# Sharing PSUM banks between small score matmuls in a fused Nyström-attention and MoE kernel

## The chip, the cores and the metric

The kernel runs on one core of one Trainium2 chip. The time is device microseconds of one execution of the whole program; the figure quoted for a kernel is the median of its runs. The engines are TensorE (PE in the rows; its weight loads are listed apart), VectorE (DVE), ScalarE (ACT), GpSimd (POOL) and the queues that issue transfers (SP above all).

## The reference, cut to what matters

Eight batches with eight heads of 576 x 64 go through Nyström attention with 32 landmarks per head, and then two gated layers without softmax follow:

```python
q_lm = q.reshape(B, H, 32, 18, D).mean(axis=3)       # landmarks: means of 18 neighbours
k_lm = k.reshape(B, H, 32, 18, D).mean(axis=3)
A  = softmax(scale * q    @ k_lm.T)                  # 576 x 32 per head
Bm = softmax(scale * q_lm @ k_lm.T)                  # 32 x 32
C  = softmax(scale * q_lm @ k.T)                     # 32 x 576
Z  = Bm.T / (norm1(Bm) * norminf(Bm) + 1e-6)
for _ in range(6):
    Z = 2 * Z - Z @ Bm @ Z                           # Newton steps
attn = A @ Z @ C @ v
x = ((attn @ w1) * (attn @ w2)) @ w3 @ w_out         # first layer
h = x @ w_in
out = elu(h) @ w_out2                                # second layer
```

All of it is float32; the large products are made of float32r halves, three matmuls for one product.

## The kernel before

The program has three stretches. In the first (to about 160 us) the weights are unpacked on ScalarE, VectorE and GpSimd (`conv_job`), a product of two weights is formed (`w3acc`), and the attention of batch 0 is worked out. In the second (to about 620 us) the first layer runs over 128 units: unit u is 12 matmuls `ab` (scores A times the folded matrix `m`) and, two units later, 12 matmuls `y`. Each has 288 columns. In the third the second layer runs (`h`, `o`), which the change doesn't touch.

In the second stretch the attention of batch b+1 is made between the units of batch b. A table of half steps, `steps`, says which piece goes where. With i the unit within a batch (0 to 15), the loop does: `ab(u)`; `quick`, which takes the Newton steps; `ab_product` (copy on ScalarE, product `g` on VectorE); `ab_split` of the unit before (`gl` on VectorE); `fill` with half step 2i; `yy(u-2)`; `fill` with half step 2i+1. So a piece at an even half step stands on TensorE between `ab` and `y`, and one at an odd half step between `y` and the next `ab`. Each engine works off its own queue in the order in which this was written. Every `fill` ends with a step of a weight conversion for the second layer (four instructions `w_y`, `w_p`, `w_p`, `w_s` on VectorE in some of the steps; products and splits on GpSimd).

The pieces that matter here, all of one batch's attention:

- `b_scores`, half step 6: landmark scores `bs`, eight small matmuls; VectorE takes the maximum (`bmx`) and the difference (`bm`). `b_exp` (7) and `b_soft` (8) finish the softmax.
- `c_scores`, 7 and 8: landmark queries against keys (`c`), each time eight matmuls of 288 columns into two PSUM banks; ScalarE copies them to `e`.
- `newton` 13 to 18 (`n`), and `cv` 18 and 19: C times v, one half of the heads each; VectorE scales both into `cvbd`.
- `zcv`, 21: Z times that (`z`), eight small matmuls, one copy on VectorE.
- `a_scores`, 22 and 26: keys' landmarks against queries (`a`), into two banks; VectorE transposes them.
- `m_tiles`, 24 and 28 (and 0 and 2 of the next batch): the matrix `m`, whose weights are `z`.

All these use one PSUM pool, `ps_at`, of two banks of 512 columns that are handed out in turn. A matmul into a bank that is handed out anew waits until the last reader of the bank's former content is done. `bs` takes 64 columns of a bank, `z` 128, a half of `c` or `a` 288.

Of the kernel before, what the change touches and what calls it, by code (L numbers as in the profile page):

```python
# [22 lines left out]
ML = 32  # L23
R = S // ML
NP = H // 2
NH = S // 2
# [36 lines left out]
def nystrom_moe_kernel(ctx, tc, qT, kT, vm, vr, w12, w3T, w_out1, w_in2, w_out2, out):  # L63
    nc = tc.nc
    pe, dve, act, pool, sp = nc.tensor, nc.vector, nc.scalar, nc.gpsimd, nc.sync
# [132 lines left out]
    qpad = att.tile([128, 2, NP, ML], F32, name="qpad")  # L198
    cvbd = att.tile([128, NP, 128], F32, name="cvbd")

    loaded = {}
# [19 lines left out]
    class Attention:  # L221
# [24 lines left out]
            for i in range(2):  # L246
                act.copy(qpad[64 * i : 64 * i + 64, i], self.qsum[64 * i : 64 * i + 64])

        def pair_scores(self, nm, small, big, cols):


            ps = [self.ps(f"{nm}{i}") for i in range(2)]
            for hp in range(NP):
                for i in range(2):
                    sl = slice(64 * i, 64 * i + 64)
                    pe.matmul(  # L256
                        ps[i][32 * hp : 32 * hp + 32, : cols.stop - cols.start],
                        small[sl, hp, :], big[sl, hp, cols], start=True, stop=True,
                    )
            return ps  # L260

        def c_scores(self, n):
            if n == 0:
                self.e = [self.t([128, S], f"e{blk}") for blk in range(2)]
            cols = slice(n * NH, (n + 1) * NH)
            for e, p in zip(self.e, self.pair_scores(f"c{n}", self.qsum, loaded[self.b]["k"], cols)):
                act.copy(e[:, cols], p[:, :NH])

        def c_max(self, blk):
# [16 lines left out]
            dve.reciprocal(self.crs.rearrange("p a o -> p (a o)"), s)  # L286

        def b_scores(self):
            p = self.ps("bs")
            for i in range(2):  # L290
                for hp in range(NP):
                    pe.matmul(
                        p[32 * hp : 32 * hp + 32, i * ML : (i + 1) * ML], qpad[:, i, hp, :], self.ksum[:, hp, :],
                        start=True, stop=True,
                    )
            pv = p[:, : 2 * ML].rearrange("p (a m) -> p a m", m=ML)
            mx = self.t([128, 2, 1], "bmx")
            dve.tensor_reduce(mx.rearrange("p a o -> p (a o)"), pv, axis=AX.X, op=ALU.max)
            bm = self.t([128, 2, ML], "bm")
            dve.tensor_tensor(bm, pv, mx.to_broadcast([128, 2, ML]), op=ALU.subtract)  # L300
            self.bm = bm

        def b_exp(self):
            act.activation(self.bm, self.bm, AF.Exp, scale=SC2)
# [94 lines left out]
                    )  # L399

        def zcv(self):
            p = self.ps("z")
            for hp in range(NP):
                for i in range(2):
                    pe.matmul(
                        p[64 * i : 64 * i + 64, hp * ML : (hp + 1) * ML], cvbd[:, hp, 64 * i : 64 * i + 64],
                        self.X[:, i, ML:], start=True, stop=True,
                    )
            self.z = self.t([128, NP, ML], "z")
            dve.tensor_copy(self.z.rearrange("p a m -> p (a m)"), p[:, : NP * ML])  # L410

        def m_tiles(self, jn):
            ps = self.pair_scores(f"m{jn}", self.z, w12_sb, slice(jn * 512, (jn + 1) * 512))
# [5 lines left out]
                M_hi[self.b, jn, blk] = hi  # L419
                M_lo[self.b, jn, blk] = lo  # L420

        def a_scores(self, n):
            t = self.t([128, 2 * SEG, ML], "at")
            tf = t.rearrange("p k m -> p (k m)")
            ps = self.pair_scores(f"a{n}", self.ksum, loaded[self.b]["q"], slice(n * NH, (n + 1) * NH))
            for blk, p in enumerate(ps):
                dve.transpose(tf[:, blk * NH : (blk + 1) * NH], p[:, :NH])
            self.at = t
# [32 lines left out]
        def steps(self, first=False):  # L461

            s = {}

            def at(i, f, *a):
                s.setdefault(i, []).append((f, a))

            for hp in range(NP):
                at((-16, -14, -12, -11)[hp], self.sums, "k", hp)
                at(hp, self.sums, "q", hp)  # L470
            at(4, self.q_pad)
            at(6, self.b_scores)
            at(7, self.b_exp)
            at(7, self.c_scores, 0)
            at(8, self.c_scores, 1)
            at(8, self.b_soft)
            at(9, self.c_max, 0)
            at(9, self.c_exp, 0)
            at(10, self.b_norms)
            at(10, self.c_max, 1)  # L480
            at(10, self.c_exp, 1)
            at(11, self.b_norms2)
            at(12, self.r0)
            at(13, self.c_norm)
            for k in range(6):
                at(13 + k, self.newton, k)
            for k in range(3):
                at(11 + 2 * k, self.c_trans, k)
            at(18, self.cv, 0)
            at(19, self.cv, 1)  # L490
            at(21, self.zcv)
            when = ((22, 22, 23, 24, 25, 26, 27), (26, 27, 28, 29, 30, 32, 34))
            if first:
                when = ((11, 11, 12, 13, 14, 15, 16), (17, 17, N1, N1 + 1, N1 + 2, N1 + 3, N1 + 4))
            for n, o in enumerate(when):
                at(o[0], self.a_scores, n)
                at(o[1], self.a_max)
                at(o[2], self.a_sub)
                at(o[3], self.a_exp)
                at(o[4], self.a_sum)  # L500
                at(o[5], self.a_mul, n)
                at(o[6], self.a_split, n)
            return s
# [6 lines left out]
    with tc.manual_schedule():  # L510
# [55 lines left out]
        for o in ORDER:  # L566
            if o == "A":
                k, n_wo = n_wo, n_wo + 1
# [25 lines left out]
        a0, st0 = atts[0], steps[0]  # L594
# [8 lines left out]
        i = 0  # L603
# [191 lines left out]
        for u in range(nu + LAG):  # L795
            if u < nu:
                b, n, fc = units[u]
                i = n * K1 + fc
# [35 lines left out]
        for u in range(LAG, n2 + LAG2):  # L834
            if u < n2:
                i, f = units2[u]
# [59 lines left out]
```

## Time and profile before

| | us |
|---|---|
| three runs | 1472.49, 1472.89, 1474.19 (median 1472.89) |
| the profiled execution | 1474.1 |
| its span | 1472.3 |
| TensorE busy | 1417.4 |
| VectorE busy | 887.3 |
| ScalarE busy | 696.1 |
| GpSimd busy | 252.4 |

TensorE is busy for 96% of the span. Its idle time lies in the first stretch; between 200 and 600 us the page shows hardly any. A busy TensorE can still lose time: matmuls are pipelined, and it is the distance between their starts that says how fast they go. VectorE is busy for some 75% of the second stretch. GpSimd works in the first two stretches alone.

### The profile page before, as it was taken

What the parts mean: (1) busy time and instruction counts of PE and PEld (TensorE: products, weight loads), DVE (VectorE), ACT (ScalarE), POOL (GpSimd) and SP (SyncE); (2) the same over time, 40 slices, a digit from 0 to 9 for tenths busy, and PEclk for the clock granted to TensorE, in tenths of its full rate; (3) what the DMA queues carried; (4) which work ended last, traced back from release to release, by engine and by line L of the source; (5) the groups of instructions that cost most, each with busy time, mean ns of one, the idle gap of its engine ahead of it and who ended that gap; (6) DMA issues with size and microseconds to landing.
All of it is one profiled execution on the core that took longest, in us unless ns stands there. A gap on an engine that the chain in (4) does not pass through costs nothing.

```text
span 1472.3 us, 23676 instructions
## 1 busy us (share of the span) xinstructions
PE 1417.4 (96%) x9552; PEld 1144.7 (78%) x9552; DVE 887.3 (60%) x1719; ACT 696.1 (47%) x1333; POOL 252.4 (17%) x231
## 2 busy tenths in 40 slices
PE   5786899999999999999999999999999999999998
PEld 2234788888888888898888888888888888888886
DVE  8988686877878786634545445454444545445443
ACT  5664444545454544334445444454444544445443
POOL 5554324243423434201000000000000000000000
PEclk9888999999999999999999999999999999999999
DMA  7553244454433333236310010100101000010000
GB/s 292 182 187 118 78 153 154 140 176 148 173 135 139 135 139 117 79 144 231 128 50 8 0 57 1 58 0 0 58 1 57 1 30 29 0 58 0 30 1 29
DMA packets 40302, 129.46 MB, mean 88 GB/s; under 512 B 3840, under 2 KB 12032, under 8 KB 35072
## 3 DMA queue, kind: packets, MB, share of 16 engines
q1 hardware_dynamic: 37888, 111.16, 21.5%
q0 software_dynamic: 2304, 16.78, 2.9%
q8 instruction: 75, 1.23, 0.3%
q14 instruction: 35, 0.29, 0.1%
HBM read 92.27 MB, written 35.65 MB: 87 GB/s over the span
## 4 chain that ended last, share of the span: by engine, by line
PE 90%; DVE 7%; issue 1%; ACT 1%; DMA 1%; SPq 0%; DVEq 0%; ACTq 0%
PE o L751 9%; PE o L753 9%; PE o L752 9%; PE h L723 9%; PE h L722 9%; PE h L724 9%; PE y L663 5%; PE ab L636 5%; PE ab L637 4%; PE ab L638 4%; PE y L665 4%; PE y L664 4%; PE m L256 2%; PE w3acc L524 2%; PE n L357 1%
## 5 line engine op out<-in xcount | busy, mean ns | idle before, releaser
L751 PE MATMUL o<-w,eh 128*128 128x512 f32 x576 | 227.0, 394 | 0.7 <-ACT ysb L669 0.7
L723 PE MATMUL h<-yl,w 128*128 128x512 f32 x576 | 227.0, 394 | 0.0
L753 PE MATMUL o<-w,el 128*128 128x512 f32 x576 | 226.9, 394 | 0.0
L752 PE MATMUL o<-w,eh 128*128 128x512 f32 x576 | 226.8, 394 | 0.0
L722 PE MATMUL h<-yh,w 128*128 128x512 f32 x576 | 226.4, 393 | 0.0
L724 PE MATMUL h<-yh,w 128*128 128x512 f32 x576 | 226.3, 393 | 0.0
L732 DVE SCALAR_TENSOR_TENSOR t<-m,t 128x512 f32<-128x512 f32 x144 | 99.7, 693 | 196.2 <-ACT m L731 196.2
L68 ACT CAST eh<-t 128x512 fp32r<-128x512 f32 x144 | 89.4, 621 | 213.7 <-DVE t L733 213.7
L663 PE MATMUL y<-gh,w3oh 128*128 128x288 f32 x512 | 160.6, 314 | 1.5 <-DVE w3ol L69 1.5
L69 DVE TENSOR_TENSOR el<-t,eh 128x512 fp32r<-128x512 f32 x144 | 99.7, 692 | 98.8 <-ACT eh L68 98.8
L636 PE MATMUL ab<-ath,mh 128*128 128x288 f32 x512 | 157.5, 308 | 1.2 <-DVE g L647 1.2
L637 PE MATMUL ab<-atl,mh 128*128 128x288 f32 x512 | 152.5, 298 | 0.0
L638 PE MATMUL ab<-ath,ml 128*128 128x288 f32 x512 | 151.8, 297 | 0.0
L665 PE MATMUL y<-gh,w3ol 128*128 128x288 f32 x512 | 151.3, 296 | 0.0
L664 PE MATMUL y<-gl,w3oh 128*128 128x288 f32 x512 | 151.2, 295 | 0.1
L728 ACT COPY hs<-h 128x512 f32<-128x512 f32 x144 | 84.4, 586 | 100.0 <-PE h L724 99.9
L751 PEld LDWEIGHTS o<-w,eh 128*128 128x128 f32 x576 | 108.2, 188 | 26.2 <-ACT ysb L669 1.1
L723 PEld LDWEIGHTS h<-yl,w 128*128 128x128 f32 x576 | 108.0, 188 | 25.6
L722 PEld LDWEIGHTS h<-yh,w 128*128 128x128 f32 x576 | 108.0, 188 | 25.4
L753 PEld LDWEIGHTS o<-w,el 128*128 128x128 f32 x576 | 108.1, 188 | 25.2
L724 PEld LDWEIGHTS h<-yh,w 128*128 128x128 f32 x576 | 108.1, 188 | 25.1
L752 PEld LDWEIGHTS o<-w,eh 128*128 128x128 f32 x576 | 108.2, 188 | 24.7
(132 smaller groups left out, 2417.2 us busy)
## 6 DMA issues: line engine op xcount, KB each, us to landing
wd<-w2c SPq DMA_DIRECT2D x32, 512.0 KB, 3.4
w<-wd POOLq DMA_DIRECT2D x16, 1024.0 KB, 14.3
k<-in_kT_dram SPq DMA_DIRECT2D x8, 1152.0 KB, 7.3
q<-in_qT_dram SPq DMA_DIRECT2D x8, 1152.0 KB, 6.1
yd<-ysb SPq DMA_DIRECT2D x16, 576.0 KB, 3.7
yin<-yd SPq DMA_DIRECT2D x36, 256.0 KB, 4.0
out_dram<-osb SPq DMA_DIRECT2D x36, 256.0 KB, 2.2
w_raw<-in_w3T_dram SPq DMA_DIRECT2D x16, 512.0 KB, 5.2
```

What stands on the lines that cost most here:

```text
L636: pe.matmul(p[:, :NH], mh[:, cs], ah[:, blk, :], start=(blk == 0), stop=False)
L637: pe.matmul(p[:, :NH], mh[:, cs], al[:, blk, :], start=False, stop=False)
L638: pe.matmul(p[:, :NH], ml[:, cs], ah[:, blk, :], start=False, stop=(blk == 1))
L663: pe.matmul(a[oc][:, :NH], w3o_hi[fc][:, os_], gh, start=(fc == 0), stop=False)
L664: pe.matmul(a[oc][:, :NH], w3o_hi[fc][:, os_], gl, start=False, stop=False)
L665: pe.matmul(a[oc][:, :NH], w3o_lo[fc][:, os_], gh, start=False, stop=(fc == K1 - 1))
L722: pe.matmul(p[:, :TB], w2[f][:, 0, kk * 128 : (kk + 1) * 128], yhi[:, kk, :], start=(kk == 0), stop=False)
L723: pe.matmul(p[:, :TB], w2[f][:, 0, kk * 128 : (kk + 1) * 128], ylo[:, kk, :], start=False, stop=False)
L724: pe.matmul(p[:, :TB], w2[f][:, 1, kk * 128 : (kk + 1) * 128], yhi[:, kk, :], start=False, stop=(kk == KD - 1))
L751: pe.matmul(a, eh[:, ts_], w2[f][:, 2, :], start=(f == 0), stop=False)
L752: pe.matmul(a, eh[:, ts_], w2[f][:, 3, :], start=False, stop=False)
L753: pe.matmul(a, el[:, ts_], w2[f][:, 2, :], start=False, stop=(f == K2 - 1))
```

## The change

Three pieces move, and two pairs of pieces share a bank.

`b_scores` no longer stands at half step 6; it is called by `c_scores(0)` at half step 7, takes the last 64 columns of a bank, and hands that bank on as the first of the two into which the keys' scores go (columns 0 to 287). `b_exp` goes from 7 to 8 and `b_soft` from 8 to 9. `cv(1)` goes from 19 to 18, right behind `cv(0)`, which stands behind the last Newton step. `zcv` goes from 21 to 22 for all batches but the first: it is called by `a_scores(0)`, takes the last 128 columns of a bank, and hands it on as the first bank of the queries' scores.

```diff
-        def pair_scores(self, nm, small, big, cols):
+        def pair_scores(self, nm, small, big, cols, ps=None):
-            ps = [self.ps(f"{nm}{i}") for i in range(2)]
+            ps = ps or [self.ps(f"{nm}{i}") for i in range(2)]
...
         def c_scores(self, n):
-            for e, p in zip(self.e, self.pair_scores(f"c{n}", self.qsum, loaded[self.b]["k"], cols)):
+            ps = [self.b_scores()] + [self.ps("c0")] if n == 0 else None
+            for e, p in zip(self.e, self.pair_scores(f"c{n}", self.qsum, loaded[self.b]["k"], cols, ps)):
...
         def b_scores(self):
             p = self.ps("bs")
+            o = 512 - 2 * ML
-                        p[32 * hp : 32 * hp + 32, i * ML : (i + 1) * ML], qpad[:, i, hp, :], self.ksum[:, hp, :],
+                        p[32 * hp : 32 * hp + 32, o + i * ML : o + (i + 1) * ML], qpad[:, i, hp, :], self.ksum[:, hp, :],
-            pv = p[:, : 2 * ML].rearrange("p (a m) -> p a m", m=ML)
+            pv = p[:, o:].rearrange("p (a m) -> p a m", m=ML)
...
+            return p
...
         def zcv(self):
-            p = self.ps("z")
+            p = self.zp = self.ps("z")
+            o = 512 - NP * ML
-                        p[64 * i : 64 * i + 64, hp * ML : (hp + 1) * ML], cvbd[:, hp, 64 * i : 64 * i + 64],
+                        p[64 * i : 64 * i + 64, o + hp * ML : o + (hp + 1) * ML], cvbd[:, hp, 64 * i : 64 * i + 64],
-            dve.tensor_copy(self.z.rearrange("p a m -> p (a m)"), p[:, : NP * ML])
+            dve.tensor_copy(self.z.rearrange("p a m -> p (a m)"), p[:, o:])
...
-        def a_scores(self, n):
+        def a_scores(self, n, with_z=False):
+            ps = None
+            if with_z:
+                self.zcv()
+                ps = [self.zp, self.ps("a0")]
-            ps = self.pair_scores(f"a{n}", self.ksum, loaded[self.b]["q"], slice(n * NH, (n + 1) * NH))
+            ps = self.pair_scores(f"a{n}", self.ksum, loaded[self.b]["q"], slice(n * NH, (n + 1) * NH), ps)
...
-            at(6, self.b_scores)
-            at(7, self.b_exp)
             at(7, self.c_scores, 0)
+            at(8, self.b_exp)
             at(8, self.c_scores, 1)
-            at(8, self.b_soft)
+            at(9, self.b_soft)
...
             at(18, self.cv, 0)
-            at(19, self.cv, 1)
-            at(21, self.zcv)
+            at(18, self.cv, 1)
+            if first:
+                at(21, self.zcv)
...
-                at(o[0], self.a_scores, n)
+                at(o[0], self.a_scores, n, not first and n == 0)
```

Three places show what this does to the queues. TensorE before, in the attention of batch 5: the product `z` stands between `y` and `ab`, the queries' scores `a` one block of `ab` later (`ath`, `mh`, `ml` are the halves of the operands of `ab`; a `w3o` row is a `y` matmul).

```order
L665 MATMUL y_5910<-gh_5737,w3ol_93 128x288
L405 MATMUL z_5923<-X_5791,cvbd 64x32 x8
L636 MATMUL ab_0_5943<-ath_5266,mh_1_0_5122 128x288
...
L638 MATMUL ab_1_5950<-ath_5266,ml_1_0_5123 128x288
L636 MATMUL ab_1_5950<-ath_5266,mh_1_1_5125 128x288
L637 MATMUL ab_1_5950<-atl_5267,mh_1_1_5125 128x288
L638 MATMUL ab_1_5950<-ath_5266,ml_1_1_5126 128x288
L256 MATMUL a_5_5966<-q_5128,ksum_4713 32x288
L256 MATMUL a_5_5967<-q_5128,ksum_4713 32x288
```

The same place on TensorE after the change, with the semaphores that each row waits for:

```order
L648 MATMUL ab_1_5929<-ath_5257,ml_1_1_5117 128x288
L411 MATMUL z_5944<-X_5781,cvbd 64x32 [waits PE_49]
L411 MATMUL z_5944<-X_5781,cvbd 64x32 x7
L256 MATMUL z_5944<-q_5119,ksum_4705 32x288 [waits DMAHW2_49,DVE_49]
L256 MATMUL a_5_5955<-q_5119,ksum_4705 32x288 [waits PE_49]
```

All 12 `ab` rows now stand ahead of `z`, nothing stands between `z` and the first score matmul, and that matmul, which writes into z's bank, waits for VectorE: the count that it waits for is the one that the copy of `z` raises. The queue of VectorE at that place, before and then after (`k` to `ksum` are the landmark sums of a later batch, `at` the transposed scores):

```order
L241 TENSOR_REDUCE ksum_5741<-k_5595 128x32
L410 COPY z_5932<-z_5923 128x128
L241 TENSOR_REDUCE ksum_5741<-k_5595 128x32
L138 TENSOR_SCALAR w_y<-w_y 128x512
L143 TENSOR_SCALAR w_p<-w_y 128x512
L146 SCALAR_TENSOR_TENSOR w_p<-w_raw,w_p 128x512
L148 TENSOR_SCALAR w_s<-w_p 128x512
L647 TENSOR_TENSOR g_5959<-ab_1_5950,a_5957 128x288
L69 TENSOR_TENSOR gl_5901<-g_5898,gh_5900 128x288
L427 STREAM_TRANSPOSE at_5965<-a_5_5966 128x288
```

```order
L241 TENSOR_REDUCE ksum_5731<-k_5585 128x32 x2
L138 TENSOR_SCALAR w_y<-w_y 128x512
L143 TENSOR_SCALAR w_p<-w_y 128x512
L146 SCALAR_TENSOR_TENSOR w_p<-w_raw,w_p 128x512
L148 TENSOR_SCALAR w_s<-w_p 128x512
L657 TENSOR_TENSOR g_5938<-ab_1_5929,a_5936 128x288
L69 TENSOR_TENSOR gl_5891<-g_5888,gh_5890 128x288
L416 COPY z_5953<-z_5944 128x128
L437 STREAM_TRANSPOSE at_5956<-z_5944 128x288
```

The copy of `z` moved behind six instructions: the four of the conversion, `g` and `gl`. On TensorE the landmark scores stand so after the change:

```order
L675 MATMUL y_5335<-gh_5252,w3ol_94 128x288
L295 MATMUL bs_5392<-ksum_4705,qpad 32x32 [waits PE_49,Activation_49]
L295 MATMUL bs_5392<-ksum_4705,qpad 32x32 x3
L295 MATMUL bs_5392<-ksum_4705,qpad 32x32 [waits Activation_49]
L256 MATMUL bs_5392<-k_4559,qsum_5196 32x288 [waits DMAHW0_49,DVE_49]
L256 MATMUL c_5_5405<-k_4559,qsum_5196 32x288 [waits PE_49]
```

Before, 12 matmuls `y` stood between the eight `bs` and the first `c`. Now the first key score follows at once and waits for the difference `bm`, the last reader of `bs`.

## Rows read from the trace of the kernel before

**Rows 1.** The page: busy tenths of TensorE, and its granted clock, in 40 slices

```profile
PE   5786899999999999999999999999999999999998
PEclk9888999999999999999999999999999999999999
```

**Rows 2.** Timeline of TensorE, batch 5's z and a: start us, us, instruction

```profile
453.51 0.29 PE L665 MATMUL y<-gh,w3ol 128*128 128x288 f32 x1
453.73 0.66 PE L405 MATMUL z<-X,cvbd 128*64 128x32 f32 x16
454.32 0.40 PE L636 MATMUL ab<-ath,mh 128*128 128x288 f32 x1
454.56 0.30 PE L637 MATMUL ab<-atl,mh 128*128 128x288 f32 x1
...
455.89 0.29 PE L638 MATMUL ab<-ath,ml 128*128 128x288 f32 x1
456.11 0.72 PE L256 MATMUL a<-q,ksum 64*32 64x288 f32 x16
```

**Rows 3.** Timeline of TensorE, batch 5's bs and the last y behind it

```profile
421.20 0.33 PE L292 MATMUL bs<-ksum,qpad 128*32 128x32 f32 x16
...
423.02 0.29 PE L665 MATMUL y<-gh,w3ol 128*128 128x288 f32 x1
```

**Rows 4.** Timeline of VectorE behind that bs

```profile
422.41 0.21 DVE L298 TENSOR_REDUCE bmx<-bs 128x2 f32<-128x64 f32 x1
422.66 0.22 DVE L300 TENSOR_TENSOR bm<-bs,bmx 128x64 f32<-128x64 f32 x1
```

**Rows 5.** Timeline of VectorE around batch 5's z: idle time before, and its releaser, in brackets

```profile
452.67 0.45 DVE L69 TENSOR_TENSOR gl<-g,gh 128x288 fp32r<-128x288 f32 x1
...
454.44 0.29 DVE L410 COPY z<-z 128x128 f32<-128x128 f32 x1 [0.66 <-PE z L405]
454.65 0.74 DVE L241 TENSOR_REDUCE ksum<-k 128x32 f32<-128x576 f32 x1
...
457.73 0.29 DVE L148 TENSOR_SCALAR w_s<-w_p 128x512 uint16<-128x512 uint16 x1
457.94 0.45 DVE L647 TENSOR_TENSOR g<-ab,a 128x288 f32<-128x288 f32 x1
458.31 1.34 DVE L69 TENSOR_TENSOR gl<-g,gh 128x288 fp32r<-128x288 f32 x1
```

**Rows 6.** Timeline of GpSimd in the same microseconds

```profile
455.52 1.29 POOL L166 TENSOR_TENSOR w2c<-w_x,w2c 128x512 fp32r<-128x512 f32 x1
458.17 1.17 POOL L155 TENSOR_TENSOR w_t<-w_t,w_s 128x512 f32<-128x512 f32 x1 [1.35 <-DVE w_s L148]
```

**Rows 7.** Timelines of VectorE and TensorE where a matmul waited for the copy of z

```profile
116.85 0.29 DVE L410 COPY z<-z 128x128 f32<-128x128 f32 x1
...
117.19 1.96 PE L256 MATMUL m<-w_sb,z 64*32 64x512 f32 x16 [3.06 <-DVE z L410]
```

**Rows 8.** Timelines of TensorE and VectorE, batch 7's a, with no conversion on VectorE

```profile
591.07 0.71 PE L256 MATMUL a<-q,ksum 64*32 64x288 f32 x16
...
591.23 0.46 DVE L647 TENSOR_TENSOR g<-ab,a 128x288 f32<-128x288 f32 x1 [1.55 <-ACT gh L68]
```

**Rows 9.** Timeline of TensorE, first m of batch 2 and of batch 3

```profile
258.31 1.45 PE L256 MATMUL m<-w_sb,z 64*32 64x512 f32 x16
...
325.75 1.09 PE L256 MATMUL m<-w_sb,z 64*32 64x512 f32 x16
```

**Rows 10.** Timeline of VectorE in the first stretch, batch 0's landmark softmax

```profile
55.22 0.21 DVE L310 TENSOR_REDUCE bsum<-bm 128x2 f32<-128x64 f32 x1
...
56.58 0.93 DVE L313 TENSOR_TENSOR bm<-bm,bsum 128x64 f32<-128x64 f32 x1
59.58 0.69 DVE L69 TENSOR_TENSOR w3ol<-w3acc,w3oh 128x512 fp32r<-128x512 f32 x1 [2.06 <-ACT w3oh L68]
```

## The prediction

> **What bounds the kernel now.** I read the page first, then TensorE's timeline through one batch, then VectorE's and GpSimd's timelines beside it. TensorE is the bound from the sixth slice on, at full granted clock (a 9 is 90% or more) [rows 1]. Within the first layer its matmuls start every 0.13 us (454.56 to 455.89 is ten steps), and small groups interrupt them. Such a group costs more than its work: the gap into it is 0.22 us (453.51 to 453.73) and the second large matmul behind it comes 0.24 us after the first, where 0.13 is usual [rows 2]. That is 0.09 + 0.11 = 0.20 us at the two edges, and it is what a merged group can save. The z group as a whole moves the stream by 454.56 - 453.51 - 0.27 = 0.78 us. VectorE is not the bound in the stretch, but it is fed by TensorE and works in order, so the question is where in its queue a result stands for which TensorE now has to wait.
>
> **What is removed.** Per batch three interruptions: bs joins c, the second half of cv joins the first, z joins a. The work of each stays. In the second stretch the first merge counts for batches 2 to 7 (batches 0 and 1 have theirs before 160 us, where TensorE waits anyway), the two others for batches 1 to 7. For cv nothing waits that did not before, so 7 x 0.20 = 1.4 us are gained. Its bounds are 0 and 0.4 per merge (a change of tile form within the group may keep an edge, or more than the edges may go).
>
> **The wait behind bs.** Before, the 12 y between bs and c (from 421.46 to 423.02) covered VectorE's maximum and difference. Now c's first matmul writes the bank that they read, and queues behind them. In the new place bs runs after those y, about 422.8 to 423.1 on this clock; VectorE had by 422.41 reached bmx, so gl and all ahead of it are done and it is idle [rows 3, 4]. From the end of the group: 0.05 to VectorE's start (z ends at 453.73 + 0.66 = 454.39, its copy starts at 454.44 [rows 2, 5]), 0.25 to the second instruction, 0.22 for it [rows 4], 0.05 back to TensorE (117.14 to 117.19 [rows 7]): 0.57 us of wait. Everything on TensorE stands behind it, the next ab first. Less the edge saved, +0.37 us a batch; six batches give +2.2 us. Bounds per batch: 0.17 (if two edges' worth is saved) and 0.57 (nothing saved).
>
> **The wait behind z.** Here VectorE is not idle. Its copy of z now stands behind the conversion's four instructions, g and gl. I work batch 5 through. TensorE, without the z group, comes to the place of the a group 0.78 us earlier: z runs from 455.33 to 455.99, and the first a could follow then. VectorE, without the 0.66 us of waiting for z and the 0.21 to its next start, has the rest of its queue 0.87 us earlier: w_s at 456.86, g at 457.07, gl at 457.44 [rows 5]. It cannot be much earlier, since GpSimd's subtraction until 456.81 holds up just this kind of instruction [rows 6]. Behind w_s's start by 0.44 us GpSimd begins its next product (458.17 against 457.73), so at 457.30, for 1.17 us; the gl row that ran beside such a product took 1.34 us, one that did not 0.45 [rows 5, 6]. I take 1.34, because four of the five gl rows at this place (batches 2 to 6) are that long. A next instruction starts 0.08 before the recorded end, so the copy runs from 458.70 to 458.99 and a starts at 459.05. The wait is 459.05 - 455.99 = 3.06 us. With a gl of 0.45 the copy would run from 457.81 and a start at 458.16: 2.17 us.
>
> Batches 2 to 5 have the same queue: three at 3.06 and one at 2.17 make 2.84, less 0.20, times four: +10.6 us. Batches 1 and 6 have their conversion elsewhere against GpSimd's work, and batch 7 has none. Its rows give the least wait there can be: g starts 0.16 us behind the old start of a (591.07 and 591.23 [rows 8]); g and gl take a step of 0.37 each, the copy 0.29, the way back 0.06, so a could start at 592.32, and z would end at 591.73: 0.59 us. With a long gl it is 1.48. I take 1.0 for batch 7, less the edge +0.8, and the middle of 0.59 and 3.06, so 1.8, for batches 1 and 6, together +3.3 (rounded up). Sum for z: +14.7 us, with bounds of 7 x 0.39 = +2.7 and 7 x 2.86 = +20.
>
> **What the waiting gives back.** The first m of a batch stands on VectorE's transposes of a. Where VectorE came late, its group took 1.45 us and not 1.09 [rows 9]; four of the batches 1 to 7 show 1.41 to 1.45. When TensorE has waited for the copy, VectorE has caught up and the transposes follow a at once: -0.35 x 4 = -1.4 us. Bounds 0 and -1.7.
>
> **The first stretch.** Batch 0's four softmax instructions ran from 55.22 to 57.51 us, in time that VectorE then spent waiting (2.06 us) for ScalarE [rows 10]. Now they stand behind that work, before the maximum that the chain of waits goes through; I take 1.0 us, between 0.8 (each at its shortest) and 2.3. In batch 1 c's start moves behind one conversion, but VectorE sets the pace there: +0.2, at most 1.3. b_exp and b_soft one half step later cost nothing in the second stretch: b_soft at 9 still stands ahead of the norms at 10, and the first matmul that needs them comes at 12, with blocks of y and ab between. No transfer is moved.
>
> **Sum.** 2.2 + 14.7 - 1.4 - 1.4 + 1.2 = +15.3 us. Made against the profiled execution's 1474.1 us (span 1472.3) this is 1489.4; that execution stood 1.2 us above the median of the runs, so on the median it is 1488.2 us. About 0.2%, 3 us, is what a measurement here can tell from no change.
>
> **Two rules of the Trainium skill.** The rows show groups of different tile forms: 128*32 for bs, 128*64 for z, 64*32 for a [rows 2, 3]. The Trainium skill, "TensorEngine Tiling (Array Packing)", section Key Properties, says that changing the tiling mode, as against the tile, drains TensorE. By it the merges bs with c and z with a save no edge, and the sum is 13 x 0.20 = 2.6 us higher; no row of before shows these two neighbours.
>
> **Rivals.** First, TensorE doesn't really wait, since the shared bank's columns are apart: then 20 merges at 0.20 give -4.0 us, with the first stretch's 1.2 on top 1470 us. Against it speak the semaphore on the first score matmul in the built program, and the copy that raises it. The Trainium skill, "PSUM — Partial Sum Buffer", section "PSUM bank collisions raise a hardware error", says that two engines collide in a bank and quadrant even at disjoint columns, so by it no such matmul can be let go early; no run here shows that. I give this 3%.
>
> Second, faster: the waits are short and the merges give back the most they can. The price is 0.4 and not 0.20 a merge, which is what a bs group of 0.33 us would set free if nearly all of it ran under c's loading. Then 20 x 0.4 = 8.0 stand against 6 x 0.57 + 7 x 0.59 = 7.5 us of waits, and with m's 1.4 us it is about 1471 us. This decides as soon as a merge saves more than half the average wait. Against it: the edges measured are 0.20. Chance 4%.
>
> Third, short waits at edges of 0.20: the conversion comes out of z's way because VectorE runs ahead, all seven waits fall to 0.59, and m still gives back a part: 2.2 + 2.7 - 1.4 - 0.5 + 1.0 = +4.0, 1477 us. If m gives back its 1.4 and the first stretch nothing, it is +2.1, and that would measure as no change. For it: VectorE no longer loses the 0.66 us ahead of z's copy. Against it: GpSimd's rows, which hold VectorE up whenever it comes. Chance 14%, of which 8 within 0.2%.
>
> Fourth, TensorE's granted clock falls after waits of 3 us, as it does in the first slices [rows 1], where waits are longer: half speed for some microseconds in each of seven batches, 1500 us or more. The slices don't show to which wait, if any, a fall belongs. Chance 4%.
>
> **How the numbers follow.** The forecast, waits of about 2 to 3 us behind z and 0.57 behind bs, has 75%. Its own range is 1480 to 1496: with gl never held up (-3.6) and batches 1 and 6 at the least wait on one side, with every wait at 3.06, and 2.3 in the first stretch, on the other. Downwards the range takes in the third rival: 1477 to 1496. Faster by over 0.2% has the first two rivals, 6% with a little of each outside; within 0.2% 9%; slower 85%.
>
> **What would show it.** In the changed kernel's waits TensorE should have a row for a behind the copy of z, seven times, some 13 to 20 us in all, the longest near 3, and one for c behind bm of about 0.57 us each in six batches. The second half of cv should start right behind the first. The first m of each batch should take 1.1 us. VectorE's copy of z should show no idle time ahead of it where a conversion is queued. I am wrong if the copy starts within 0.1 us of z's end, if a long gl doesn't stand ahead of it, or if the edges of the groups that are left have become longer.

## The result, and the profile after

| | us |
|---|---|
| before, median of four runs | 1473.26 (1472.49 to 1474.19) |
| after, median of four runs | 1492.44 (1492.27 to 1492.95) |
| ratio | 1.0131, 95% interval 1.0113 to 1.0148 |
| forecast | 1488.2 (1477 to 1496) |
| span of the profiled execution, before and after | 1472.3 and 1490.6 |

The changed kernel is slower by 1.3%, some 19 us. The forecast of +15 us had the sign and nearly the size, but the time is not made up as it said. The page after has nearly the same two lines as [rows 1]: TensorE's busy share and its granted clock both stand at 9, 90% or more, from the fifth slice to the last but one. One execution of a kernel below, the one with z in a bank of its own, took 3563.9 us where its three others took 1486.5 to 1487.9; it is left out.

```profile
PE   5785999999999999999999999999999999999998
PEclk9888999999999999999999999999999999999999
```

The waits say more. The columns are who waited for whom, us in total, times, the longest. This is TensorE between 180 and 615 us, in the second stretch, first before and then after:

```profile
PE m L256 <- DVE at L427: 0.2, 1, 0.2
```

```profile
PE z L256 <- DVE z L416: 8.7, 7, 2.4
PE ct L372 <- ACT e L278: 8.4, 6, 1.4
PE bs L256 <- DVE bm L303: 3.6, 6, 0.6
```

The first and third row were forecast. The second was not: `ct` is the transpose of the exponentiated key scores `e` (`c_trans(0)`, half step 11), and nothing in the diff touches it.

To see where each wait counts I took, from TensorE's timeline, the start of the first `ab` of every unit and compared the distances from one unit to the next, before and after. Outside the rows below they agree within 0.15 us, most of them within 0.02.

| part | where | after less before, us | sum | forecast |
|---|---|---|---|---|
| bs with c | unit 3 | +0.50 in each of six batches | +3.0 | +2.2 |
| ct | unit 5 | +1.60 in each of six batches | +9.6 | 0 |
| z with a | units 10 and 11, without the 0.10 that cv saves there | +1.0 in five batches, +2.3 and +0.45 | +7.8 | +14.7 |
| cv in one | units 9 and 10 | -0.06 and -0.10 in each of seven | -1.1 | -1.4 |
| m no longer late | units 12 and 14 | -0.45, -0.35, -0.31, -0.60 and four of about -0.09 | -2.1 | -1.4 |
| first stretch, to unit 8 of batch 0 | | first `ab` 123.70 and 126.77, then -2.2 | +0.9 | +1.2 |

With 0.2 for the few units left over, that is the +18.3 of the two spans.

The rows that answer to [rows 3, 4], TensorE and VectorE at batch 5's bs after the change. The bracket is the idle time before and its releaser. The sixteen matmuls of `c` are listed under the tile whose bank they write, `bs` or `c`:

```profile
432.38 0.33 PE L295 MATMUL bs<-ksum,qpad 128*32 128x32 f32 x16
433.31 0.43 PE L256 MATMUL bs<-k,qsum 64*32 64x288 f32 x1 [0.61 <-DVE bm L303]
...
432.78 0.22 DVE L301 TENSOR_REDUCE bmx<-bs 128x2 f32<-128x64 f32 x1 [0.70 <-PE bs L295]
433.04 0.22 DVE L303 TENSOR_TENSOR bm<-bs,bmx 128x64 f32<-128x64 f32 x1
```

VectorE was idle, as forecast, and the wait is 0.61 us where 0.57 was worked out.

The rows that answer to [rows 2, 5, 6], TensorE, VectorE and GpSimd at batch 3's z, which stands for five of the seven:

```profile
326.92 0.66 PE L411 MATMUL z<-X,cvbd 128*64 128x32 f32 x16
328.74 0.43 PE L256 MATMUL z<-q,ksum 64*32 64x288 f32 x1 [1.16 <-DVE z L416]
...
327.41 0.29 DVE L148 TENSOR_SCALAR w_s<-w_p 128x512 uint16<-128x512 uint16 x1
327.62 0.45 DVE L657 TENSOR_TENSOR g<-ab,a 128x288 f32<-128x288 f32 x1
327.99 0.49 DVE L69 TENSOR_TENSOR gl<-g,gh 128x288 fp32r<-128x288 f32 x1
328.41 0.28 DVE L416 COPY z<-z 128x128 f32<-128x128 f32 x1
...
327.45 0.72 POOL L165 CAST w2c<-w_x 128x512 fp32r<-128x512 f32 x1 [5.64 <-DMA wd<-w2c]
328.25 1.36 POOL L166 TENSOR_TENSOR w2c<-w_x,w2c 128x512 fp32r<-128x512 f32 x1
```

VectorE has no idle time between the conversion and the copy, as forecast. But `gl` took 0.49 us and not 1.34: GpSimd's subtraction (L166) began 0.26 us behind it. In batch 5 alone it was the other way round, and there the wait is 2.39 us. The two differ by little: in batch 3 `w_s` starts 0.04 us ahead of GpSimd's cast (L165) and takes 0.29 us, in batch 5 0.08 us behind it (467.60 and 467.52) and takes 0.68.

```profile
468.20 0.45 DVE L657 TENSOR_TENSOR g<-ab,a 128x288 f32<-128x288 f32 x1
468.56 1.22 DVE L69 TENSOR_TENSOR gl<-g,gh 128x288 fp32r<-128x288 f32 x1
469.71 0.28 DVE L416 COPY z<-z 128x128 f32<-128x128 f32 x1
...
468.21 1.26 POOL L166 TENSOR_TENSOR w2c<-w_x,w2c 128x512 fp32r<-128x512 f32 x1
```

Now the wait for `e`. VectorE in batch 5 before, with the landmark softmax (`bsum`, `bm`) ahead of the conversion:

```profile
426.60 0.21 DVE L310 TENSOR_REDUCE bsum<-bm 128x2 f32<-128x64 f32 x1
426.84 0.17 DVE L311 TENSOR_SCALAR bsum<-bsum 128x2 f32<-128x2 f32 x1
...
427.24 0.22 DVE L313 TENSOR_TENSOR bm<-bm,bsum 128x64 f32<-128x64 f32 x1
...
428.76 0.29 DVE L148 TENSOR_SCALAR w_s<-w_p 128x512 uint16<-128x512 uint16 x1
428.97 0.75 DVE L273 TENSOR_REDUCE cb<-e 128x1 f32<-128x576 f32 x1
```

And after, VectorE, GpSimd and TensorE:

```profile
438.05 0.30 DVE L148 TENSOR_SCALAR w_s<-w_p 128x512 uint16<-128x512 uint16 x1
438.26 0.21 DVE L314 TENSOR_REDUCE bsum<-bm 128x2 f32<-128x64 f32 x1
438.51 1.17 DVE L315 TENSOR_SCALAR bsum<-bsum 128x2 f32<-128x2 f32 x1
...
439.91 1.06 DVE L317 TENSOR_TENSOR bm<-bm,bsum 128x64 f32<-128x64 f32 x1
440.90 0.74 DVE L274 TENSOR_REDUCE cb<-e 128x1 f32<-128x576 f32 x1
...
438.49 1.16 POOL L155 TENSOR_TENSOR w_t<-w_t,w_s 128x512 f32<-128x512 f32 x1 [3.35 <-DVE bsum L314]
439.73 1.16 POOL L161 TENSOR_TENSOR w_x<-w_t,w_p 128x512 f32<-128x512 f32 x1
...
442.84 0.66 PE L372 MATMUL ct<-ident,e 128*128 128x128 f32 x4 [1.40 <-ACT e L278]
```

Before, the maximum of `e` (`cb`) started 0.21 us behind `w_s`. Now the four softmax instructions lie between them, and it starts 2.85 us behind. They are no longer 0.8 us long either: `w_s` is what GpSimd's next product (L155) reads (its row after names `bsum`, which ended just ahead of its start), so they now run beside GpSimd, and two of them are held until its instruction is done (438.51 + 1.17 = 439.68 against 438.49 + 1.16 = 439.65, and again at 440.97 and 440.89). The exponential and the transposes stand behind the maximum. This is the mechanism behind [rows 10] in the first stretch (0.93 us for `bm`; the second of those four instructions, 0.88 us long, ends there at 56.35 and GpSimd's at 56.32), and the one that the prediction used for `gl`. The Trainium skill, "SBUF — State Buffer", section "Who interferes with whom", tells of an exclusive lock between the two engines that is held for a whole instruction; these ends agree with it to 0.1 us.

### The profile page after: what moved, and what is told of

Same layout as the page of the kernel before. It is cut to its first block, busy times and chain, and to the rows that moved or that the text cites. A ratio compares the mean times of both kernels' runs of the same rounds, so it can differ in the third digit from the quotient of the medians.

```text
span 1490.6 us, 23677 instructions
## 1 busy us (share of the span) xinstructions
PE 1410.5 (95%) x9552; PEld 1140.7 (77%) x9552; DVE 892.2 (60%) x1719; ACT 695.4 (47%) x1333; POOL 250.3 (17%) x231
## 4 chain that ended last, share of the span: by engine, by line
PE 86%; DVE 10%; ACT 1%; issue 1%; DMA 0%; DVEq 0%; SPq 0%; ACTq 0%
PE o L761 9%; PE o L762 9%; PE o L763 9%; PE h L733 9%; PE h L732 9%; PE h L734 9%; PE y L673 5%; PE ab L646 4%; PE ab L647 4%; PE ab L648 4%; PE y L675 4%; PE y L674 4%; PE m L256 2%; DVE w_p L146 1%; PE w3acc L534 1%
```

## Experiments

The theory to be tested: the loss is three separate waits, and the largest comes from an order on VectorE, not from the shared banks. Times stand against the runs of the kernel before on the same chip (medians 1473.4 to 1474.2 us).

**The softmax behind the maximum.** One edit to the changed kernel:

```diff
-            at(9, self.b_soft)
             at(9, self.c_max, 0)
             at(9, self.c_exp, 0)
+            at(9, self.b_soft)
```

> The changed kernel with one edit: in half step 9 the softmax of the landmark scores (b_soft) is queued behind c_max(0) and c_exp(0) instead of ahead of them. Theory A (queue order): of the 19.2 us that the change cost, about 9.6 are the wait of the score transposes ct at half step 11 (1.38 us in most batches), because four small operations of b_soft now stand between the conversion's last operation and the maximum that the exponential needs; with the order turned that wait goes, 1492.4 - 9.6 = 1482.8 us (1481 to 1485). Rival B (shared banks only): e is late because the c scores themselves come later behind bs, and the order on VectorE does not matter: 1492 us within 0.2%, ct still waits over 1 us.

1486.9 us, ratio to before 1.0094 (1.0080 to 1.0107). Its waits between 180 and 615 us:

```profile
PE z L256 <- DVE z L416: 9.0, 7, 2.4
PE bs L256 <- DVE bm L303: 3.7, 6, 0.6
PE n L361 <- ACT ct L377: 1.7, 6, 0.5
```

The wait for `e` is gone, unit 5 is as long as before, and bs still shares its bank: so the order was the cause, and rival B falls. But the gain is 5.6 us and not 9.6. Part of it came back one unit later, 0.33 us in each batch at the Newton start `n`, which now waits in its turn (by this row for the copy of `ct`, in the run with both edits, below, for VectorE's `X`); another part, in the profiled execution, is the clock: 1.4 us in batch 5, and most of 1.9 us in batch 1, where the wait behind z was also 0.35 us longer (1.48; below). That execution took 1489.5 us, 2.7 more than the median.

**The softmax half a step later in the kernel before.** Nothing merged, only this:

```diff
-            at(7, self.b_exp)
             at(7, self.c_scores, 0)
+            at(8, self.b_exp)
             at(8, self.c_scores, 1)
-            at(8, self.b_soft)
+            at(9, self.b_soft)
```

> The kernel before with one part of the change alone: b_exp at half step 8 and b_soft at half step 9 (the landmark scores stay at half step 6 in a bank of their own, nothing is merged). Theory A: this part alone costs the wait of ct: 1473.3 + 9.6 = 1482.9 us (1481 to 1485). Rival B: it costs nothing without the shared banks, 1473 us within 0.2%.

1484.1 us, ratio 1.0070 (1.0057 to 1.0083): +10.2 us. By units it is the kernel before within 0.15 us from batch 1 on, but for unit 5 with +1.59 to +1.63 in six batches, and this row in the waits:

```profile
PE ct L368 <- ACT e L277: 8.4, 6, 1.4
```

In unit 5 both directions give the same number, 1.6 us a batch, so half of what the change costs has nothing to do with sharing banks.

**Readers behind all writers of a bank.** In the changed kernel the two reads move behind the score matmuls (`b_read` holds `bmx` and `bm`, `z_read` the copy of z, both taken out of `b_scores` and `zcv`):

```diff
         def c_scores(self, n):
-            for e, p in zip(self.e, self.pair_scores(f"c{n}", self.qsum, loaded[self.b]["k"], cols, ps)):
+            ps = self.pair_scores(f"c{n}", self.qsum, loaded[self.b]["k"], cols, ps)
+            if n == 0:
+                self.b_read()
+            for e, p in zip(self.e, ps):
                 act.copy(e[:, cols], p[:, :NH])
...
         def a_scores(self, n, with_z=False):
...
             ps = self.pair_scores(f"a{n}", self.ksum, loaded[self.b]["q"], slice(n * NH, (n + 1) * NH), ps)
+            if with_z:
+                self.z_read()
             for blk, p in enumerate(ps):
```

> The changed kernel with both reads of a shared bank queued behind all the matmuls that write it: bmx and bm are issued behind the 16 matmuls of c(0), the copy of z behind the 16 of a(0), so that no matmul has to wait for VectorE inside a group. Theory A: the waits behind z (8.7 us in the trace) and bs (7.2 us without batch 0's) go, the wait of ct (9.3 us) stays: 1492.4 - 15.9 + up to 4 for the later readers = 1476.5 to 1481 us, ct still waiting over 1 us per batch. Rival B: all of the 19.2 us come from the shared banks: 1473 us or less, ct no longer waiting. Rival C: the wait is only passed on, the c copies, the m tiles or the transposes of a come as much later: over 1488 us.

1479.0 us, ratio 1.0037 (1.0024 to 1.0051). In the second stretch one wait of TensorE is left, a little longer than in the changed kernel:

```profile
PE ct L379 <- ACT e L281: 10.5, 6, 1.8
```

One wait has moved to ScalarE. Its first copy of `e`, out of the bank that bs shares, now stands behind `bm`; in each of the six batches it starts 1.06 to 1.07 us behind the start of the last `c` matmul, where it was 0.49 in the changed kernel. Batch 5:

```profile
427.02 0.40 ACT L271 COPY e<-bs 128x288 f32<-128x288 f32 x1 [3.13 <-DVE bm L311]
```

Units 3 are now 0.18 us shorter than before the change, units 10 and 11 together 0.31. The waits on TensorE were not passed on at anything like their size (rival C), and they are not all of the loss (rival B).

**Both edits.**

> The edits of the two runs before this one together: readers of a shared bank behind all its matmuls, and b_soft behind c_max(0) and c_exp(0). Theory A: neither wait is left, the interruptions saved per batch (two beginnings and ends of 0.20 us, and the m tiles no longer late by 0.2 to 0.6 us) remain: 1473.3 - 7 x 0.40 - 1.7 = 1468.8 us (1466 to 1473). Rival B: no more than the late readers alone, within 1 us of that run. Rival C: the waits are passed on: over 1480 us.

1467.7 us, ratio 0.9964 (0.9951 to 0.9976): faster than the kernel before. Batch 5 shows well why. TensorE and VectorE at its z:

```profile
450.48 0.66 PE L418 MATMUL z<-X,cvbd 128*64 128x32 f32 x16
451.06 0.43 PE L256 MATMUL z<-q,ksum 64*32 64x288 f32 x1
...
452.05 1.25 DVE L69 TENSOR_TENSOR gl<-g,gh 128x288 fp32r<-128x288 f32 x1
453.22 0.28 DVE L426 COPY z<-z 128x128 f32<-128x128 f32 x1
```

The copy comes as late as in the changed kernel, 2.7 us behind z's start there and here, with the same long `gl`. But TensorE no longer cares. The loss lay in where the read stands in program order, not in the read's own lateness.

**One part undone: z in a bank of its own.** `zcv` at 21 in all batches, `a_scores(0)` with two banks of its own.

> The changed kernel with one part undone: the z scores stay at half step 21 in a bank of their own and a(0) takes two banks of its own, in all batches. Theory A: the wait for the copy of z goes (in the trace 0.9 us net in most batches, 2.2 in one, 0.35 in the last, 7.1 in sum), and the m tiles are late again as in the kernel before (1.7 us in sum): 1492.4 - 7.1 + 1.7 = 1487.0 us (1485 to 1489). Rival: as predicted, 13 to 16 us of the change hang on z: 1477 to 1481 us.

1487.1 us, ratio 1.0094 (1.0079 to 1.0110): 5.3 us less than the changed kernel, as the trace said and not as the prediction did. Two of the first m groups are 0.28 us longer than before the change.

**One part undone: bs in a bank of its own.** `b_scores` at 6, `b_exp` and `b_soft` as changed.

> The changed kernel with one part undone: the landmark scores bs stay at half step 6 in a bank of their own, c(0) in half step 7 takes two banks of its own; b_exp stays at 8 and b_soft at 9. Theory A: the bs part alone is worth 0.50 us per batch in six batches, 3.0 us, and up to 4 us in the first stretch, where the changed kernel waits 4.0 us behind bs once: 1492.4 - 3.0 - (0 to 3) = 1486.5 to 1489.5 us, ct still waits 1.4 us per batch. Rival: ct waits because bs shares its bank, and both waits go: 1480 us or less.

1491.1 us, ratio 1.0118 (1.0103 to 1.0134). The six batches give the 0.50 us each, and `ct` waits on. The sum missed the interval: the first stretch gave nothing, and batch 5 cost 1.4 us more in the profiled execution, through the clock.

**One part alone: both cv halves in half step 18.**

```diff
             at(18, self.cv, 0)
-            at(19, self.cv, 1)
+            at(18, self.cv, 1)
```

> The kernel before with one part of the change alone: cv(1) stands in half step 18 directly behind cv(0). Theory A (as predicted): one interruption less per batch at 0.20 us each, 1473.9 - 1.4 = 1472.5 us, units 9 of the batches shorter by 0.20 us. Theory B (from the trace of the changed kernel, where these units are shorter by 0.06 us): the edge between the halves stays inside the merged group, because the last chunk of a half has 64 rows and the others 128, and the array pauses 0.15 us at each such change: 1473.9 - 0.4 = 1473.5 us.

1474.3 us, ratio 1.0006 (0.9997 to 1.0015): no difference that the runs can tell. The units can: -0.06 in unit 9 and -0.10 in unit 10 of every batch, 0.16 in all, nearer to theory A than unit 9 alone had suggested. In this profile the first `ab` comes 1.6 us later and two of the first m groups are 0.28 us longer, which hides the 1.1 us.

**Edges inside cv.** Two more edits stand on the late readers. One takes the softmax to where it was before the change (`b_exp` at 7 behind the copies of c(0), `b_soft` at 8); the other starts cv's second half with its chunk of 64 rows:

```diff
-            for c in range(5):
+            order = ((0, 1, 2, 3, 4), (4, 0, 1, 2, 3))[blk]
+            for c in order:
```

> The changed kernel with readers of a shared bank behind all its matmuls, and the softmax of the landmark scores one half step earlier: b_exp at 7 behind the copies of c(0), b_soft at 8, ahead of the conversion's operations. Theory A: the wait of ct is gone as with b_soft behind c_max (1467.7 us), and the wait of the Newton start (n, 0.43 us per batch there, since b_norms came later) is gone too: 1467.7 - 6 x 0.43 = 1465.1 us (1463.5 to 1467). Rival: b_exp stands in the way of ScalarE's copies in half step 7 and the product of the next unit comes late: 1468 us or more.

1468.6 us, ratio 0.9969 (0.9958 to 0.9979). The wait of `n` is gone, but `ct` starts 0.28 us later in each batch. A miss, with the rival's number. The likely cause of most of it is `b_exp`, which now stands between the copies and the conversion on ScalarE; in the last kernel below, where it stands behind them, 0.1 us is left. That rest may come from the later copy of `e`, which all kernels with late readers have; no run separates the two.

> The run before this one with the second half of cv started by its chunk of 64 rows, so that the two chunks of 64 rows stand side by side: two changes between 128 and 64 rows fewer per batch. Theory B of the cv merge: each change costs 0.15 us where the next matmuls of one form follow in 0.04 us, so 2 x 0.11 x 8 = 1.8 us less than the run before it (1.4 to 2.0), with units 9 shorter by 0.22 us. Rival: the pause belongs to the change of halves, not of rows, and nothing is saved: within 0.4 us of it.

1467.3 us, ratio 0.9960 (0.9947 to 0.9972). The group of 80 matmuls, in the changed kernel and here:

```profile
458.75 1.73 PE L390 MATMUL cv<-v,ct 128*32 128x64 f32 x80
```

```profile
443.97 1.60 PE L398 MATMUL cv<-v,ct 128*32 128x64 f32 x80
```

It is 0.13 us shorter per batch. So part of an edge does stay inside the merged group, at the changes between chunks of 128 and of 64 rows: there the next matmul starts 0.15 us behind the last. The 0.22 expected counted two changes fewer, but within the group three became two, and one at 0.11 is near the 0.13 measured. The other was meant to go at the group's end, where the first `y` follows 0.15 us behind the last `cv` in either order.

**The pieces together.** Late readers, the 64-row chunks side by side, `b_exp` first and `b_soft` last in half step 8 (in batch 0 `b_soft` in 9 behind `c_exp`).

> The changed kernel with readers of a shared bank behind all its matmuls, cv's chunks of 64 rows side by side, and the softmax of the landmark scores split over one half step: b_exp first in 8, b_soft last in 8 (in the first batch b_soft in 9 behind c_max and c_exp). Theory: ct's wait of 0.28 us per batch in the run with b_exp in 7 came from b_exp standing ahead of the conversion on ScalarE; behind the next unit's copy it delays nothing, and the wait of n (0.43 us) does not come back: against the kernel before -0.19 (bs) -0.19 (cv) -0.31 (z) -0.25 (m) = -0.94 us per batch in six batches and -3.7 in the first stretch as with b_soft behind c_max, 1473.4 - 9.3 = 1464.1 us (1462.5 to 1466). Rival: the first stretch comes out differently each time that something near it moves, and the sum is 1466 to 1468.

1467.2 us, ratio 0.9953 (0.9941 to 0.9966): 7.0 us faster than before, but not the 1464.1 expected. The six batches give -4.3 where -5.6 was expected (`ct` still +0.1), the first stretch -1.3 and not -3.7. (Here the first stretch takes in all of batch 0.) The profiled execution took 1468.5 us, 1.4 more than the median, and it is the one profile in which the granted clock stood at 0.95 for most of the time up to 478 us; from batch 1 to there units that this kernel leaves alone are up to 0.06 us longer, so its -4.3 is somewhat too small. The kernel can't be told from the other three with late readers and no wait for `e` (1467.3 to 1468.6); what the second stretch gains among them is of the size by which the first one moves.

**The same two kernels again.**

> The kernel before, unchanged, profiled a second time, to see how far its first stretch (up to the first ab matmul, 123.70 us in the first profile) repeats. Theory: the first stretch moves with DMA arrivals from one execution to the next, so that the first ab lies anywhere from 122.5 to 126.5 us, while the distances between units behind it repeat within 0.1 us. Rival: it repeats within 0.3 us, and the differences of the first stretch seen between the kernels belong to the kernels.

> The changed kernel, unchanged, profiled a second time: first ab at 126.77 us in the first profile, 15.25 us more than before from there to the first h. Theory: the first ab moves by over 1 us, the units from batch 1 on repeat within 0.1 us, apart from the wait behind z in batch 5, where GpSimd's subtraction falls on gl or does not. Rival: everything repeats within 0.3 us.

Before: first `ab` at 122.60 us, where it was 123.70, batch 0 then 0.6 us shorter, and all units of batches 1 to 6 within 0.04 us. After: first `ab` at 125.14, where it was 126.77; the units of batches 1 to 6 repeat within 0.1 us, with one exception. Batch 5's z costs 1.4 us more, though its wait is the same 2.4 us. The stretches around it, after again and then after (columns: stretch, length, busy time of TensorE, weight loads, VectorE, ScalarE, GpSimd, granted clock, share of the DMA engines, GB/s):

```profile
467.50:470.00 2.50, 0.53 (x16) 0.41 (x15) 2.47 (x4) 0.00 (x0) 2.04 (x3) 1.00 0.01 3
470.00:471.00 1.00, 0.60 (x16) 0.23 (x16) 0.35 (x2) 0.00 (x0) 1.00 (x1) 0.60 0.33 131
471.00:472.00 1.00, 1.00 (x18) 0.45 (x3) 0.30 (x1) 0.00 (x0) 0.92 (x2) 0.50 1.11 381
472.00:473.00 1.00, 1.00 (x6) 1.00 (x6) 0.97 (x3) 0.00 (x0) 0.40 (x1) 0.50 0.58 176
```

```profile
469.60:470.60 1.00, 0.56 (x16) 0.18 (x16) 0.39 (x2) 0.00 (x0) 1.00 (x1) 1.00 0.30 123
470.60:471.60 1.00, 1.00 (x15) 0.91 (x8) 0.75 (x2) 0.00 (x0) 0.92 (x2) 1.00 1.06 377
```

After the wait the granted clock is 0.50 in the one execution, 1.2 GHz, and 1.00 in the other.

## Why the prediction was near, and where it was wrong

**The frame held.** TensorE is the bound, and the two waits that were forecast are on its path, each with the releaser that was named. Of the rivals, no wait and merges worth 0.4 us each fell. The third, short waits because VectorE runs ahead, came halfway: the conversion still stands ahead of the copy, but `gl` is held in one batch only, and the waits behind z come to 8.7 us, with five near 1.1, where the prediction named 13 to 20 as its sign.

**"b_exp and b_soft one half step later cost nothing in the second stretch" failed.** It is the largest single term, +9.6 us, shown from both sides. The step looked for who needs the softmax (the norms at 10, the first matmul at 12) and found room. It didn't ask what is queued behind it: at half step 9 the maximum of `e` comes next on VectorE, and the block of y that seemed to lie between is exactly what TensorE has run out of when `ct` comes. And it took no new price for the four instructions, though they moved across `w_s`, which lets GpSimd start. For the first stretch the prediction did both, and its 1.2 us came out near 0.9, though that stretch repeats only within 1 to 2 us.

**The wait behind z had the right cause and the wrong size:** +7.8 for +14.7. The term that failed is the long `gl`, forecast in three of four batches and found in one of the four. The prediction carried GpSimd's place over from the kernel before. Its own sign of being wrong, that no long `gl` stands ahead of the copy, came true in six of the seven batches. GpSimd's cast (L165) waits for a transfer of spilled weights, which is issued on SP behind the store of y, and in batches 3 to 5 it starts 4.77 to 4.79 us behind that store in either kernel (in batch 2 4.90 before and 7.01 after). Batch 3 before, SP and GpSimd:

```profile
315.65 0.52 SPq L671 DMA_DIRECT2D yd<-ysb  x1
...
320.43 0.61 POOL L165 CAST w2c<-w_x 128x512 fp32r<-128x512 f32 x1 [4.77 <-DMA wd<-w2c]
```

And after:

```profile
322.67 0.53 SPq L681 DMA_DIRECT2D yd<-ysb  x1
...
327.45 0.72 POOL L165 CAST w2c<-w_x 128x512 fp32r<-128x512 f32 x1 [5.64 <-DMA wd<-w2c]
```

On TensorE the way from that store to the first score matmul's place got shorter: the second cv half (in batch 5 before, from the last y at 449.30 to the second ab at 450.58 less 0.27, the reckoning that gave z's 0.78: 1.0 us) went from behind the y that is stored to ahead of it, and z (0.78 us) went to the end of the way. VectorE's queue came earlier by that and more: in batch 3 `w_s` starts 7.68 us behind the store before (323.33) and 4.74 after. 1.8 us of these 2.9 are TensorE's; 1.0 is an instruction of the conversion (`w_p`) that ran beside GpSimd's subtraction before, 1.27 us long, and now runs ahead of it in 0.29. So `gl` was mostly through first. "No transfer is moved" was true of the queue and wrong of the clock: the work between a transfer and its neighbour was moved. Batches 1 and 6, put at 1.8, waited 1.1 as well; batch 7, put at 1.0 above a least of 0.59, waited 0.58. In the run with both edits, where nothing waits, the cast starts 0.53 us behind z's first matmul in batch 3 as here, so the waits are not what shifted it.

**The wait behind bs was right:** 0.61 measured, 0.57 forecast. The batch pays 0.50, since 0.11 of the edge came back and not the 0.20 taken.

**The edges were right.** Without waits bs with c saves 0.18 us a batch, and z with a 0.31, of which 0.10 are cv's; cv saves 0.16. All stand for 0.20. The Trainium skill's rule in "TensorEngine Tiling (Array Packing)", Key Properties, that a change of tiling mode drains TensorE, is borne out by the shorter cv group. What the prediction drew from it, that bs with c and z with a would then save nothing, is not: a pause between the groups stays, but one way into and out of the large stream goes.

**m** gave back 2.1 for 1.4: all four late groups are now like this one, and a second group per batch, not counted, gave 0.09 in four.

```profile
262.82 1.09 PE L256 MATMUL m<-w_sb,z 64*32 64x512 f32 x16
```

**The clock** was a rival at 4%, for waits of 3 us in seven batches. The waits of 0.6 to 1.8 us in these kernels left it at 1.00, but for one: behind the 1.48 us of batch 1 with the softmax behind the maximum it fell to 0.50 for some 3 us. TensorE's timeline there and the stretch behind it, in the columns above:

```profile
190.77 0.43 PE L256 MATMUL z<-q,ksum 64*32 64x288 f32 x1 [1.48 <-DVE z L416]
...
192.00:193.00 1.00, 1.00 (x6) 1.00 (x5) 0.97 (x3) 0.00 (x0) 0.92 (x2) 0.50 0.55 221
```

Behind the wait of 2.4 us it fell in three of the four profiles that have it (the second one of the changed kernel, the softmax behind the maximum, bs apart), for some 3 us at 0.50, at a price of 1.4 us. That is too small for the rival's 1500 us. What decides whether such a wait is followed by a fall is open.

So 1488.2 was near 1492.4 by luck, because two errors stood against each other: 9.6 us not seen, and 6.9 too many at z. The range held; the working did not earn it. The forecast's own lower end, 1480, is also not what its terms give: 3.6 for `gl` and 2.4 for batches 1 and 6 lead from 1488.2 to 1482.2, and the 3.6 takes `gl` as held in four batches where the sum has three.

**Left open.** Whether the chip itself would need the waits at the shared banks was not tried, since a kernel without them would have a race. What moves the first stretch by 1 to 2 us from one execution to the next was not followed. It is enough to hide the second stretch's gains below 2 us.

## What to carry to other kernels

When a step is moved on an engine that works in order, ask what is queued behind its new place, and which other engine was released just ahead of it; that the step's own reader has time says nothing of either. Two groups of matmuls can share a bank without a wait of TensorE if all writes are issued before the first read, and only then is a merge worth its edge (here about 0.2 us); a second reader of the bank can still come later (here ScalarE's copy, by 0.6 us). A transfer's neighbours keep its time, not the program's: when work between them moves, what runs beside what changes too.

## What was not expected of the hardware

- Instructions on two columns, 0.17 us alone, took 1.17 us beside GpSimd: on VectorE even a very small instruction can last until GpSimd's current one is done.
- A matmul group keeps a pause at each change between 128 and 64 rows within itself; putting two such chunks side by side took 0.13 us off a group of 1.73.
- After an idle time of 2.4 us TensorE's granted clock fell to 0.50 in three profiles and stayed at 1.00 in one, with the same instructions around it. It also fell once after 1.48 us, and stayed at 1.00 after six waits of 1.7 to 1.8 us in another kernel.
